# Second layer: turning the mixed rows of tiles 4 to 11 on VectorE and through DRAM instead of on TensorE

## The chip, the cores and the metric

The kernel runs on one core of one Trainium2 chip. The core has five engines that run their own instruction streams in program order: TensorE (PE in the rows), VectorE (DVE), ScalarE (ACT), GpSimd (POOL) and SyncE (SP), which here only issues DMAs. ScalarE can issue DMAs too. Transfers run on 16 DMA engines, beside the compute engines. The metric is the device time of one execution in microseconds (us); lower is better.

## What is computed

The reference chains three layers over 1536 rows (2 batches of 768) of width 512: a retention attention, a mixture of 8 experts with two experts for each row, and the layer that the change touches, called the second layer here. Cut to what matters, with `x` the weighted sum of the two experts' results for each row:

```python
x = top2_w[:, 0, None] * y0 + top2_w[:, 1, None] * y1      # the mixed rows
h = x @ w_in                                               # 512 -> 1024
e = np.exp(h - h.max(-1, keepdims=True))
solu = h * e / (e.sum(-1, keepdims=True) + 1e-9)
ln = (solu - mean(solu)) / np.sqrt(var(solu) + 1e-6) * g_ln
out = ln @ w_out                                           # 1024 -> 512
```

All of it is float32; the kernel gets there by splitting each operand into a high and a low part and adding three products.

## The kernel before

The second layer works on 12 tiles of 128 rows (`NT = 12`). For tile i it takes these steps, each a small function:

- `gather(i)`: GpSimd fetches the two experts' rows of the tile by two indirect DMAs from `yg` into `y0` and `y1` (L801).
- `mix(i)`: ScalarE scales `y0` (L811), VectorE adds the scaled `y1` (L812); the result `t` has a row of the tile in each partition.
- `x2_t(i)`: TensorE turns `t` by four 128x128 transposes into PSUM (L821), so that the width lies in the partitions; ScalarE writes the high part `x2h` (L824), VectorE the low part `x2l` (L825).
- `h_in(i, s)`, s = 0 and 1: 24 matmuls of 512 columns in all, `h` into PSUM bank pair `d` (L840). The first two matmuls read `x2h`, the third reads `x2l`.
- `solu_max(i)`: VectorE takes the row maximum (L845) and negates it (L846). `solu(i)`: ScalarE's exponential (L853), VectorE's product (L854), three short steps, and `z` (L859).
- `z_turn(i)`: VectorE turns the 32x32 blocks of `z` (L904, into `zs`); four DMAs on SyncE's queue store `zs` to DRAM (`zd`, L907); a fifth, behind them on the same queue, loads it back with the blocks in their places (`zc`, L909). It can start when the four stores have landed. Tiles 0 and 11 are turned on TensorE instead (`z_t`, L893).
- `z_parts(i)`: ScalarE and VectorE make the high and low parts `zh` and `zl` from `zc` (L916, L917).
- `RS[i]()`: ScalarE's sum of squares (L864) and six short GpSimd steps for the row's scale.
- `out_mm(i)`: 24 matmuls of 512 columns (L950), 16 with `zh` first. `store_out(i)`: ScalarE scales and evacuates (L956, tile `o`), SyncE stores to the output (L957).

The order of every engine's instructions is the order in which the program calls these functions; no scheduler moves them. An instruction that waits holds what stands behind it on its engine, and a DMA that waits holds its queue. A prologue brings the first tiles in; then a loop runs over i = 1 to 11. Its body before the change, cut to the calls, with the tile that each works on:

```python
store_out(i - 1); x2_t(i + 3); mix(i + 4); gather(i + 5); z_parts(i)
RS[i + 1]() ; h_in(i + 2, 0); h_in(i + 2, 1)
solu_max(i + 2); solu(i + 2); z_turn(i + 2); out_mm(i)
```

So one pass of the loop gives TensorE the transposes of tile i+3, `h_in` of tile i+2 and `out_mm` of tile i. The prologue ends with `x2_t(3)`, `mix(4)`, `solu_max(2)`, `solu(2)`, `z_turn(2)`, the row scale of tile 1 and `out_mm(0)`.

Of the kernel before, what the change touches and what calls it, by code (L numbers as in the profile page):

```python
# [8 lines left out]
F32 = mybir.dt.float32  # L9
F32R = mybir.dt.float32r  # L10
# [5 lines left out]
AF = mybir.ActivationFunctionType  # L16
# [26 lines left out]
def retnet_moe_solu(ctx, tc, qT, kT, k, v, w_gate, w_noise, noise, w1, w2, w_in, w_out, g_ln,  # L43
                    decay, out, dbg=None):
    nc = tc.nc
# [3 lines left out]
    NT = B * NC  # L49
    E = w1.shape[0]  # L50
    DM = H * D
    KD = DM // 128
# [9 lines left out]
    dram = ctx.enter_context(tc.tile_pool(name="dram", bufs=1, space=DRAM))  # L62
# [10 lines left out]
    def bank(tag, shape=(128, 512)):  # L73
        if tag == "a" and tag not in psum:
            turned[0] ^= 1
            tag = f"a{turned[0]}"
        pool, n = psum[tag]
        return pool.tile(list(shape), F32, tag=tag, name=tag, bufs=n)
# [63 lines left out]
    def row0(i):  # L142
        c, b = order[i]
        return b * S + c * 128
# [646 lines left out]
    Y, X2, X2T, PH, ST, Z, RS, ZT = {}, {}, {}, {}, {}, {}, {}, {}  # L791
# [3 lines left out]
    def gather(i, upto=OFF[-1]):  # L795
        if i >= NT:
            return
        Y[i] = []
        for s in range(2):
            t = fr.tile([128, DM], F32, tag=f"y{s}", name=f"y{s}", bufs=3)  # L800
            nc.gpsimd.indirect_dma_start(  # L801
                out=t, out_offset=None, in_=yg[:upto],
                in_offset=bass.IndirectOffsetOnAxis(ap=slot_y[:, i, s:s + 1], axis=0))
            Y[i].append(t)

    def mix(i):
        if i >= NT:
            return
        y0, y1 = Y.pop(i)
        t = fr.tile([128, DM], F32, tag="t", name="t")  # L810
        nc.scalar.activation(t, y0, AF.Copy, scale=top_w[:, i, 0:1])  # L811
        nc.vector.scalar_tensor_tensor(t, y1, top_w[:, i, 1:2], t, op0=OP.mult, op1=OP.add)  # L812
        X2[i] = t

    def x2_t(i):
        if i >= NT:
            return
        t = X2.pop(i)
        p = bank("a")
        for d in range(KD):  # L820
            nc.tensor.transpose(p[:, d * 128:(d + 1) * 128], t[:, d * 128:(d + 1) * 128], ident)  # L821
        hi = fr.tile([128, KD * 128], F32R, tag="x2h", name="x2h")
        lo = fr.tile([128, KD * 128], F32R, tag="x2l", name="x2l")
        nc.scalar.activation(hi, p, AF.Copy)  # L824
        nc.vector.tensor_sub(lo, p, hi)  # L825
        X2T[i] = (hi, lo)

    def h_in(i, s):
        if i >= NT:
            return  # L830
        if s == 0:
            PH[i] = bank(f"d{i % 2}", (128, 2, 512))
        hi, lo = X2T[i]
        f = slice(s * 512, s * 512 + 512)
        terms = [(x, d, n) for d in range(KD) for x, n in ((hi, 0), (hi, 1), (lo, 0))]
        if s == 0 and i == 0:

            terms.sort(key=lambda t: t[0] is lo)
        for m, (x, d, n) in enumerate(terms):
            nc.tensor.matmul(PH[i][:, s, :], x[:, d * 128:(d + 1) * 128], unit_t[8 * E + d][n][:, 0, f],  # L840
                             start=(m == 0), stop=(m == len(terms) - 1))

    def row_max(pool, ph):
        t = pool.tile([128, 16], F32, tag="st", name="st", bufs=3)
        nc.vector.reduce_max(t[:, 0:1], ph, axis=AX.X)  # L845
        nc.vector.tensor_scalar_mul(t[:, 0:1], t[:, 0:1], -1.0)  # L846
        return t

    def solu_rows(pool, ph, t):

        col = lambda n: t[:, n:n + 1]
        ee = pool.tile([128, FF], F32, tag="ee", name="ee")
        nc.scalar.activation(ee, ph, AF.Exp, bias=col(0), accum_out=col(1))  # L853
        nc.vector.scalar_tensor_tensor(ee, ph, 1.0, ee, op0=OP.mult, op1=OP.mult, accum_out=col(2))  # L854
        nc.vector.tensor_scalar_add(col(1), col(1), 1e-9)
        nc.vector.reciprocal(col(3), col(1))
        nc.vector.scalar_tensor_tensor(col(4), col(2), 1.0 / FF, col(3), op0=OP.mult, op1=OP.mult)
        z = pool.tile([128, FF], F32, tag="z", name="z")
        nc.vector.tensor_scalar(z, ee, col(3), col(4), op0=OP.mult, op1=OP.subtract)  # L859
        return z, lambda: row_scale(ee, z, t)  # L860
# [14 lines left out]
    def solu_max(i):  # L875
        if i >= NT:
            return
        ST[i] = row_max(m2, PH[i].rearrange("p a f -> p (a f)"))

    def solu(i):  # L880
        if i >= NT:
            return
        Z[i], RS[i] = solu_rows(m2, PH.pop(i).rearrange("p a f -> p (a f)"), ST.pop(i))
# [17 lines left out]
    def z_turn(i):  # L901

        t = m2.tile([128, 4, 256], F32, tag="zs", name="zs")
        nc.vector.transpose(t.rearrange("p g c -> p (g c)"), Z.pop(i).rearrange("p (k g c) -> p g k c", g=4, c=32))  # L904
        d = dram.tile([4, 32, 4, 256], F32, tag="zd", name="zd", bufs=3)
        for a in range(4):
            nc.sync.dma_start(d[:, :, a].rearrange("g i c -> i g c"), t[32 * a:32 * a + 32])  # L907
        t = m2.tile([128, 4, KF, 32], F32, tag="zc", name="zc")
        nc.sync.dma_start(t, d.rearrange("g i a (k j) -> (g i) a k j", j=32))  # L909
        ZD[i] = t  # L910

    def z_parts(i):
        hi = m2.tile([128, KF, 4, 32], F32R, tag="zh", name="zh")
        lo = m2.tile([128, KF, 4, 32], F32R, tag="zl", name="zl")
        t = ZD.pop(i).rearrange("p a k j -> p k a j")
        nc.scalar.activation(hi, t, AF.Copy)  # L916
        nc.vector.tensor_sub(lo, t, hi)  # L917
        ZT[i] = tuple(x.rearrange("p k a j -> p (k a j)") for x in (hi, lo))
# [24 lines left out]
    def out_mm(i, c=slice(0, DM), between=None):  # L943
        hi, lo = ZT[i]
        p = bank("b")[:, c]
        terms = [(z, f, n) for z, ns in ((hi, (0, 1)), (lo, (0,))) for f in range(KF) for n in ns]
        for m, (z, f, n) in enumerate(terms):
            if between and m == len(terms) // 2:
                between()
            nc.tensor.matmul(p, z[:, f * 128:(f + 1) * 128], w_rows(f, n)[:, c],  # L950
                             start=(m == 0), stop=(m == len(terms) - 1))
        OUT[i] = p

    def store_out(i, c=slice(0, DM)):
        o = m2.tile([128, DM], F32, tag="o", name="o", bufs=3)
        nc.scalar.activation(o[:, c], OUT.pop(i), AF.Copy, scale=RS[i])  # L956
        nc.sync.dma_start(out[row0(i):row0(i) + 128, c], o[:, c])  # L957

# [128 lines left out]
    for e in range(E - 1):  # L1087
# [5 lines left out]
        for j in range(4):  # L1093
            for f in (2 * j, 2 * j + 1):
                hidden(e, f, slice(0 if e else EARLY, CAPS[e]))
                if f in (1, 3, 4, 5):
                    d = (1, 3, 4, 5).index(f)
# [66 lines left out]
    fr = m2_ctx.enter_context(tc.tile_pool(name="fr", bufs=2, side="right", reuse_waits="tile"))  # L1164
    for b in range(3):
        py = bank(("c0", "c3", "c2")[b])
        c = slice(b * 128, (b + 1) * 128)
# [15 lines left out]
    m2 = m2_ctx.enter_context(tc.tile_pool(name="m2", bufs=2, reuse_waits="tile"))  # L1183
    psum_pool(m2_ctx, "psum2", a=2, b=2, d0=1, d1=1)
    gather(3)
    gather(4)
    h_in(0, 0)
    x2_t(1)
    h_in(0, 1)
    mix(2)  # L1190
    solu_max(0)
    solu(0)
    x2_t(2)
    h_in(1, 0)
    h_in(1, 1)
    mix(3)
# [9 lines left out]
    mix(4)  # L1206
    gather(5)
    solu_max(2)
    solu(2)
    z_turn(2)  # L1210
    RS[1] = RS[1]()
    out_mm(0)

    for i in range(1, NT):
        store_out(i - 1)
        x2_t(i + 3)
        mix(i + 4)
        gather(i + 5)
        if i < NT - 2:
            z_parts(i)  # L1220
        if i + 1 < NT:
            RS[i + 1] = RS[i + 1]()
        h_in(i + 2, 0)
        h_in(i + 2, 1)
        solu_max(i + 2)
        solu(i + 2)
        if i + 2 < NT - 1:
            z_turn(i + 2)
        if i == NT - 3:
            z_parts(i + 1)  # L1230
        if i < NT - 1:
            out_mm(i, between=(lambda: z_t(NT - 1)) if i == NT - 2 else None)
        else:
            for c in (slice(0, DM // 2), slice(DM // 2, DM)):
                out_mm(i, c)
                store_out(i, c)
# [5 lines left out]
    with tc.If(full == 1), ExitStack() as fb_ctx:  # L1242
        fb = fb_ctx.enter_context(tc.tile_pool(name="fb", bufs=1))
        psum_pool(fb_ctx, "psum3", a=2, b=2, d0=1)
        for g in range(NT // 4):
            xT = fb.tile([128, KD, 4, 128], F32, tag="fx", name="fx")
            acc, gate = [], []
            for n in range(4):
                i = 4 * g + n
                x = fb.tile([128, DM], F32, tag="fr", name="fr")  # L1250
                nc.sync.dma_start(x, xd[i * 128:(i + 1) * 128, :])
                p = bank("a")
# [9 lines left out]
                a = fb.tile([128, DM], F32, tag=f"fa{n}", name="fa")  # L1262
# [10 lines left out]
            for e in range(E):  # L1273
                wa, wb = load_w(w1[e], w2[e])
                h = fb.tile([128, KF, 512], F32, tag="fh", name="fh")
                for f in range(KF):
                    p = bank("b")
# [5 lines left out]
                for n in range(4):  # L1283
                    p = bank("a")
# [6 lines left out]
            for n in range(4):  # L1291
                i = 4 * g + n
                x2T = fb.tile([128, DM], F32, tag="fr", name="fr")
                p = bank("a")
# [12 lines left out]
                for f in range(KF):  # L1307
                    p = bank("a", (128, 128))
                    nc.tensor.transpose(p, z[:, f * 128:(f + 1) * 128], ident)
                    nc.vector.tensor_scalar_mul(zT[:, f], p, gcol[:, f:f + 1])  # L1310
                p = bank("b")
                for f in range(KF):
                    nc.tensor.matmul(p, zT[:, f], wb[:, f], start=(f == 0), stop=(f == KF - 1))
                o = fb.tile([128, DM], F32, tag="fo", name="fo")
# [57 lines left out]
```

## Time and profile before

| | us |
|---|---|
| median of 3 runs | 509.22 |
| lowest and highest run | 509.2 and 509.84 |
| the profiled execution | 509.66 |
| span in the profile, first to last instruction | 507.8 |
| TensorE busy, of the span | 499.9 (98%) |
| VectorE busy | 370.9 (73%) |
| ScalarE busy | 214.6 (42%) |
| GpSimd busy | 152.8 (30%) |

The profile is of one execution, 0.44 us above the median; 1.86 us of its time lie around the span. Times in the views are from the span's start. The second layer's first transposes stand at 361 us, and the loop over i runs from 387.1 us to the end. An engine's busy share says how much it works, not whether it is waited for: for that the views to read are the chain of work that ended last, and for each engine the idle time before an instruction with what ended it. DMA issues stand in the rows under the engine whose queue issues them (SPq, ACTq); the time in such a row is that of issuing, not that of the transfer.

### The profile page before, as it was taken

The numbers are of one execution on the slowest core, as the hardware profiler recorded it, in microseconds if no ns is written. First come the engines' busy times: TensorE is split into PE (matmuls) and PEld (weight loads), VectorE is DVE, ScalarE is ACT, GpSimd is POOL, SyncE is SP. The second block draws the span as 40 slices with busy tenths as digits, with TensorE's granted clock in tenths as the row PEclk, the third lists the DMA queues.
The fourth block names the chain that finished last, engine by engine and source line by source line (L and its number), as shares of the span: only waits on it lengthen the run. The fifth ranks groups of instructions, "written<-read, shape, count | busy, mean of one in ns | idle before, by whom it ended". The sixth has DMA issues, their size and how long they took to land.

```text
span 507.8 us, 8812 instructions
## 1 busy us (share of the span) xinstructions
PE 499.9 (98%) x3188; PEld 453.6 (89%) x3188; DVE 370.9 (73%) x744; ACT 214.6 (42%) x424; POOL 152.8 (30%) x225
## 2 busy tenths in 40 slices
PE   9999999999999999999999999999999999999995
PEld 8888888989999999999999999998788888888885
DVE  4578787679789688687889888875288766666540
ACT  5756424244424334423444444354365443344441
POOL 4111111878317127037046000000426442211120
PEclk9999999999999999999999999999999999999999
DMA  8999652977567567766587857664734765533431
GB/s 298 288 342 300 218 180 75 319 234 264 141 222 238 136 216 246 215 221 232 146 257 237 252 172 230 184 174 143 233 100 135 220 198 179 160 103 105 119 110 48
DMA packets 58962, 100.14 MB, mean 197 GB/s; under 512 B 9856, under 2 KB 27264, under 8 KB 58912
## 3 DMA queue, kind: packets, MB, share of 16 engines
q1 hardware_dynamic: 52032, 84.87, 53.4%
q0 software_dynamic: 4992, 13.25, 8.8%
q10 hardware_dynamic: 1888, 1.39, 1.0%
q8 instruction: 27, 0.44, 0.4%
q14 instruction: 23, 0.19, 0.1%
HBM read 76.81 MB, written 22.68 MB: 196 GB/s over the span
## 4 chain that ended last, share of the span: by engine, by line
PE 95%; DVE 3%; DMA 1%; issue 0%; ACT 0%; DVEq 0%; ACTq 0%
PE c L1075 25%; PE b L707 15%; PE d L840 13%; PE b L950 13%; PE a L707 12%; PE c L1173 3%; PE b L403 3%; PE c L457 3%; PE c L445 2%; PE a L431 1%; PE c L420 1%; PE a L821 1%; DMA kt<-in_kT_dram 1%; PE a L1034 0%; DVE hl L712 0%
## 5 line engine op out<-in xcount | busy, mean ns | idle before, releaser
L1021 POOL DMA_INDIRECT xq<-xd,rows x78 | 90.2, 1156 | 96.0 <-DVE xt L1038 73.4
L1075 PE MATMUL c<-hh,wh 128*128 128x448 f32 (+5 forms) x224 | 79.1, 353 | 0.0
L1075 PE MATMUL c<-hl,wh 128*128 128x448 f32 (+5 forms) x224 | 78.9, 352 | 0.0
L1075 PE MATMUL c<-hh,wl 128*128 128x448 f32 (+5 forms) x224 | 78.8, 352 | 0.0
L202 DVE TENSOR_TENSOR wl<-wr,wh 128x1024 fp32r<-128x1024 f32 x64 | 76.7, 1219 | 0.8 <-ACT wh L201 0.8
L201 ACT ACTIVATE wh<-wr 128x1024 fp32r<-128x1024 f32 x64 | 65.4, 1049 | 0.0
L801 POOL DMA_INDIRECT y<-yg,slot_y x24 | 23.5, 978 | 88.0 <-DMA yg<-y 77.3
L1075 PEld LDWEIGHTS c<-hh,wh 128*128 128x128 f32 x224 | 42.2, 188 | 1.3
L1075 PEld LDWEIGHTS c<-hh,wl 128*128 128x128 f32 x224 | 42.1, 188 | 1.2
L1075 PEld LDWEIGHTS c<-hl,wh 128*128 128x128 f32 x224 | 42.1, 188 | 1.2
L1040 ACT ACTIVATE xh<-xt 128x428 fp32r<-128x428 f32 (+5 forms) x24 | 13.0, 540 | 62.0 <-DVE xt L1038 62.0
L711 ACT ACTIVATE hh<-b 128x256 fp32r<-128x256 f32 (+8 forms) x40 | 18.7, 467 | 48.4 <-PE b L707 41.6
L707 PE MATMUL b<-xh,wh 128*128 128x448 f32 (+6 forms) x112 | 39.1, 349 | 0.0
L840 PE MATMUL d<-wh,x2h 128*128 128x512 f32 x96 | 39.0, 407 | 0.0
L707 PE MATMUL a<-xh,wh 128*128 128x448 f32 (+6 forms) x112 | 39.0, 348 | 0.0
L707 PE MATMUL b<-xh,wl 128*128 128x448 f32 (+6 forms) x112 | 38.8, 347 | 0.0
L707 PE MATMUL a<-xh,wl 128*128 128x448 f32 (+6 forms) x112 | 38.8, 347 | 0.0
L840 PE MATMUL d<-wl,x2h 128*128 128x512 f32 x96 | 37.9, 395 | 0.0
L840 PE MATMUL d<-wh,x2l 128*128 128x512 f32 x96 | 37.4, 395 | 0.0
L711 ACT ACTIVATE hh<-a 128x448 fp32r<-128x448 f32 (+6 forms) x28 | 14.3, 512 | 46.7 <-PE a L707 32.7
L853 ACT ACTIVATE ee<-d,st 128x1024 f32<-128x1024 f32 x12 | 13.4, 1114 | 40.4 <-DVE st L846 37.3
L712 DVE SCALAR_TENSOR_TENSOR hl<-b,hh 128x256 fp32r<-128x256 f32 (+8 forms) x40 | 21.0, 524 | 8.2 <-ACT hh L711 6.5
(230 smaller groups left out, 1075.6 us busy)
## 6 DMA issues: line engine op xcount, KB each, us to landing
wr<-in_moe_w_dram SPq DMA_DIRECT2D x62, 512.0 KB
zd<-zs SPq DMA_DIRECT2D x40, 128.0 KB
zc<-zd SPq DMA_DIRECT2D x10, 512.0 KB
raw<-in_moe_w_in_dram SPq DMA_DIRECT2D x8, 512.0 KB
raw<-in_moe_w_out_dram SPq DMA_DIRECT2D x8, 512.0 KB
yg<-yr SPq DMA_DIRECT2D x16, 208.0 KB
qt<-in_qT_dram SPq DMA_DIRECT2D x12, 256.0 KB
vt<-in_v_dram SPq DMA_DIRECT2D x12, 256.0 KB
```

Of the source, the lines that this page charges most:

```text
L201: nc.scalar.activation(hi, t, AF.Copy)
L202: nc.vector.tensor_sub(lo, t, hi)
L403: nc.tensor.matmul(p[s][:, hp, :], KT[i][r, hp, :], QT[i][r, hp, :], start=True, stop=True)
L457: nc.tensor.matmul(rows[:, at:at + 128 + 2 * E], XT[i][:, s, k, :], unit[:, s, k, :], start=(k == 0), stop=(k == 1), skip_group_check=True)
L707: nc.tensor.matmul(p, w[:, 0, f * 128:(f + 1) * 128], x[:, d, c], start=(n == 0), stop=(n == len(terms) - 1))
L711: nc.scalar.activation(hh[:, f, c], p, AF.Relu)
L712: nc.vector.scalar_tensor_tensor(hl[:, f, c], p, 0.0, hh[:, f, c], op0=OP.max, op1=OP.subtract)
L801: nc.gpsimd.indirect_dma_start(out=t, out_offset=None, in_=yg[:upto], in_offset=bass.IndirectOffsetOnAxis(ap=slot_y[:, i, s:s + 1], axis=0))
L840: nc.tensor.matmul(PH[i][:, s, :], x[:, d * 128:(d + 1) * 128], unit_t[8 * E + d][n][:, 0, f], start=(m == 0), stop=(m == len(terms) - 1))
L950: nc.tensor.matmul(p, z[:, f * 128:(f + 1) * 128], w_rows(f, n)[:, c], start=(m == 0), stop=(m == len(terms) - 1))
L1021: nc.gpsimd.indirect_dma_start(out=x[:, b], out_offset=None, in_=xd.rearrange("r (a c) -> (r a) c", a=4), in_offset=bass.IndirectOffsetOnA ...
L1075: nc.tensor.matmul(py[d][:, :CAPS[e]], c, h[:, f, :CAPS[e]], start=(f == 0 and n == 0), stop=(f == KF - 1 and n == 2))
```

## The change

The transposes of `x2_t` leave TensorE for tiles 4 to 11; tiles 0 to 3 keep them. In their place stand four functions, built like `z_turn` and `z_parts`: `x_turn` (VectorE turns the 32x32 blocks of `t` into `xs`), `x_store` (four DMAs on ScalarE's queue, `xs` to DRAM tile `xt`), `x_fetch` (one DMA on SyncE's queue, `xt` to `xc`) and `x_parts` (ScalarE and VectorE make `x2h` and `x2l`, now from SBUF). `xs` and `xc` have one buffer each; `o` loses one of three.

```diff
+    def x_turn(i):
+        t = m2.tile([128, 4, 128], F32, tag="xs", name="xs", bufs=1)
+        nc.vector.transpose(t.rearrange("p g c -> p (g c)"), X2.pop(i).rearrange("p (k g c) -> p g k c", g=4, c=32))
+        XS[i] = t
+    def x_store(i):
+        t = XS.pop(i)
+        d = dram.tile([4, 32, 4, 128], F32, tag="xt", name="xt", bufs=3)
+        for a in range(4):
+            nc.scalar.dma_start(d[:, :, a].rearrange("g i c -> i g c"), t[32 * a:32 * a + 32])
+        XD[i] = d
+    def x_fetch(i):
+        t = m2.tile([128, 4, KD, 32], F32, tag="xc", name="xc", bufs=1)
+        nc.sync.dma_start(t, XD[i].rearrange("g i a (k j) -> (g i) a k j", j=32))
+        XD[i] = t
+    def x_parts(i):
+        hi = fr.tile([128, KD, 4, 32], F32R, tag="x2h", name="x2h")
+        lo = fr.tile([128, KD, 4, 32], F32R, tag="x2l", name="x2l")
+        t = XD.pop(i).rearrange("p a k j -> p k a j")
+        nc.scalar.activation(hi, t, AF.Copy)
+        nc.vector.tensor_sub(lo, t, hi)
+        X2T[i] = tuple(x.rearrange("p k a j -> p (k a j)") for x in (hi, lo))
...
     def store_out(i, c=slice(0, DM)):
-        o = m2.tile([128, DM], F32, tag="o", name="o", bufs=3)
+        o = m2.tile([128, DM], F32, tag="o", name="o", bufs=2)
...
     solu_max(2)
+    x_turn(4)
     solu(2)
+    x_store(4)
     z_turn(2)
+    x_fetch(4)
     RS[1] = RS[1]()
     out_mm(0)
 
     for i in range(1, NT):
         store_out(i - 1)
-        x2_t(i + 3)
         mix(i + 4)
         gather(i + 5)
         if i < NT - 2:
             z_parts(i)
+        x_turn(i + 4)
         if i + 1 < NT:
             RS[i + 1] = RS[i + 1]()
+        x_store(i + 4)
         h_in(i + 2, 0)
         h_in(i + 2, 1)
         solu_max(i + 2)
+        x_parts(i + 3)
         solu(i + 2)
+        x_fetch(i + 4)
         if i + 2 < NT - 1:
             z_turn(i + 2)
```

SyncE's queue, from the turn of tile 1 in the prologue to the first stores of tile 3 in the loop's first pass. Before (`zd` and `zc` are the DRAM copy of `z` and its way back, `out_dram` the output):

```order
L907 DMA zd<-zs 32x4x256 x4
L909 DMA zc<-zd 128x1024
L907 DMA zd<-zs 32x4x256 x4
L909 DMA zc<-zd 128x1024
L957 DMA out_dram<-o 128x512
L907 DMA zd<-zs 32x4x256 x4
```

and now, the same stretch (`xc<-xt` is `x_fetch`, first of tile 4, then of tile 5):

```order
L943 DMA zd<-zs 32x4x256 x4
L945 DMA zc<-zd 128x1024
L943 DMA zd<-zs 32x4x256 x4
L945 DMA zc<-zd 128x1024
L851 DMA xc<-xt 128x512
L993 DMA out_dram<-o 128x512
L851 DMA xc<-xt 128x512
L943 DMA zd<-zs 32x4x256 x4
```

The fetch of tile 4 stands behind the stores and the load of `z` of tile 2; the fetch of tile 5 stands behind the first output store and ahead of the stores of tile 3.

ScalarE, from the exponential of tile 2 in the prologue to the exponential of tile 3 in the loop's first pass. Before (`ee,st<-d` is the exponential, `ee,st<-z` the sum of squares, `t<-y` the first half of `mix`):

```order
L853 ACTIVATE ee,st<-d_4401,st 128x1024
L864 ACTIVATE ee,st<-z 128x1024
L956 ACTIVATE o<-b,st 128x512
L824 ACTIVATE x2h<-a 128x512
L811 ACTIVATE t<-y_4445,top_w 128x512
L916 ACTIVATE zh<-zc 128x1024
L864 ACTIVATE ee,st<-z 128x1024
L853 ACTIVATE ee,st<-d_4531,st 128x1024
```

and now:

```order
L889 ACTIVATE ee,st<-d_4401,st 128x1024
L844 DMA xt<-xs 32x4x128 x4
L900 ACTIVATE ee,st<-z 128x1024
L992 ACTIVATE o<-b,st 128x512
L811 ACTIVATE t<-y_4445,top_w 128x512
L952 ACTIVATE zh<-zc 128x1024
L900 ACTIVATE ee,st<-z 128x1024
L844 DMA xt<-xs 32x4x128 x4
L860 ACTIVATE x2h<-xc 128x512
L889 ACTIVATE ee,st<-d_4538,st 128x1024
```

The stores of tile 4 stand ahead of the sum of squares of tile 1, those of tile 5 behind the sum of squares of tile 2, and the high part of tile 4, which reads the fetched `xc`, stands ahead of the exponential of tile 3.

## Rows read from the trace of the kernel before

**Rows 1.** The page: the chain that ended last, by engine.
```profile
PE 95%; DVE 3%; DMA 1%; issue 0%; ACT 0%; DVEq 0%; ACTq 0%
```

**Rows 2.** Chain in order of time, loop's start and last transposes: start, us, work.
```profile
387.10 0.44 PE a L821 x4
...
393.13 5.50 PE b L950 x24
398.63 0.44 PE a L821 x4
399.07 5.59 PE d L840 x24
...
467.83 0.44 PE a L821 x4
```

**Rows 3.** Timeline of SyncE's DMA issues: start, us, line, transfer, count.
```profile
392.03 1.74 SPq L907 DMA_DIRECT2D zd<-zs  x4
397.13 0.34 SPq L909 DMA_DIRECT2D zc<-zd  x1
...
422.92 1.76 SPq L907 DMA_DIRECT2D zd<-zs  x4
426.62 0.34 SPq L909 DMA_DIRECT2D zc<-zd  x1
...
484.30 0.34 SPq L909 DMA_DIRECT2D zc<-zd  x1
```

**Rows 4.** Timeline of ScalarE: loop's first two passes, and tile 10's parts.
```profile
386.94 1.12 ACT L853 ACTIVATE ee<-d,st 128x1024 f32<-128x1024 f32 x1 [4.04 <-DVE st L846]
388.05 1.05 ACT L864 ACTIVATE ee<-z 128x1024 f32<-128x1024 f32 x1
...
390.75 1.06 ACT L916 ACTIVATE zh<-zc 128x1024 fp32r<-128x1024 f32 x1
...
402.16 1.06 ACT L916 ACTIVATE zh<-zc 128x1024 fp32r<-128x1024 f32 x1 [1.65 <-DMA zc<-zd]
...
488.19 1.06 ACT L916 ACTIVATE zh<-zc 128x1024 fp32r<-128x1024 f32 x1 [0.40 <-DMA zc<-zd]
```

**Rows 5.** Timeline of ScalarE at the kernel's start: first of four DMA issues, next instruction.
```profile
0.74 0.41 ACTq L237 DMA_DIRECT2D kt<-in_kT_dram  x1
...
2.71 1.28 ACT L336 ACT_TABLE_LOAD   x1 [2.71 <-issue]
```

**Rows 6.** Timeline of VectorE: tile 2 in the prologue, then one steady pass.
```profile
386.69 0.15 DVE L846 TENSOR_SCALAR st<-st 128x1 f32<-128x1 f32 x1
...
390.75 1.25 DVE L904 STREAM_TRANSPOSE zs<-z 128x1024 f32<-128x1024 f32 x1
...
430.60 1.23 DVE L854 SCALAR_TENSOR_TENSOR ee<-d,ee 128x1024 f32<-128x1024 f32 x1 [1.35 <-ACT ee L853]
...
433.18 1.25 DVE L904 STREAM_TRANSPOSE zs<-z 128x1024 f32<-128x1024 f32 x1
```

**Rows 7.** Groups by line, 398.6 to 479.4 us: busy us, mean ns, idle before.
```profile
L917 DVE TENSOR_TENSOR zl<-zc,zh 128x1024 fp32r<-128x1024 f32 x7 | 8.6, 1226 | 2.4 <-ACT zh L916 2.4
```

**Rows 8.** Stretches: length, busy PE, PEld, DVE, ACT, POOL, PEclk, DMA share, GB/s.
```profile
8.00:12.00 4.00, 4.00 (x70) 3.54 (x66) 2.14 (x4) 3.87 (x19) 0.79 (x2) 1.00 1.04 388
387.10:398.63 11.53, 11.53 (x54) 9.40 (x53) 8.86 (x17) 6.95 (x12) 7.54 (x16) 1.00 0.62 181
```

**Rows 9.** Stretches after TensorE's last matmul, the same columns.
```profile
502.60:505.20 2.60, 0.00 (x0) 0.00 (x0) 0.00 (x0) 0.45 (x1) 0.00 (x0) 1.00 0.19 63
505.40:507.80 2.40, 0.00 (x0) 0.00 (x0) 0.00 (x0) 0.00 (x0) 0.00 (x0) 0.50 0.01 3
```

**Rows 10.** Timeline of TensorE: first matmuls, and the same 16 later.
```profile
1.05 3.38 PE L264 MATMUL c<-ones 128*128 128x128 bf16 x30 [1.05 <-DVE ones L261]
4.59 2.08 PE L403 MATMUL b<-qt,kt 64*128 64x128 f32 x16 [0.15 <-DMA kt<-in_kT_dram]
...
17.64 1.16 PE L403 MATMUL b<-qt,kt 64*128 64x128 f32 x16
```

More of the change, by code (lines that the diff above doesn't have):

```diff
@@ L826, in x2_t @@
         X2T[i] = (hi, lo)
+    XS, XD = {}, {}
+    def x_turn(i):
+        if i >= NT:
+            return
+        t = m2.tile([128, 4, 128], F32, tag="xs", name="xs", bufs=1)
+        nc.vector.transpose(t.rearrange("p g c -> p (g c)"), X2.pop(i).rearrange("p (k g c) -> p g k c", g=4, c=32))
+        XS[i] = t
+    def x_store(i):
+        if i >= NT:
+            return
+        t = XS.pop(i)
[4 more added lines that the diff above has]
+    def x_fetch(i):
+        if i >= NT:
+            return
+        t = m2.tile([128, 4, KD, 32], F32, tag="xc", name="xc", bufs=1)
+        nc.sync.dma_start(t, XD[i].rearrange("g i a (k j) -> (g i) a k j", j=32))
+        XD[i] = t
+    def x_parts(i):
+        if i >= NT:
+            return
+        hi = fr.tile([128, KD, 4, 32], F32R, tag="x2h", name="x2h")
[4 more added lines that the diff above has]
+        X2T[i] = tuple(x.rearrange("p k a j -> p (k a j)") for x in (hi, lo))
     def h_in(i, s):
```

## The prediction

> **What bounds the kernel now.** I read first the chain that ended last. TensorE has 95% of it [rows 1]: work taken from TensorE can shorten the kernel, and a TensorE wait lengthens it, one for one. Next, the same chain in order of time over the second layer [rows 2]: the reader should see matmuls standing end to end, with 0.44 us of transposes between one pass's `out_mm` and the next pass's `h_in`. From the loop's start on TensorE waits for nothing; a pass is 0.44 + 5.59 + 5.50 = 11.53 us. Then the queues of the engines that will feed `h_in` instead: SyncE's issues [rows 3], ScalarE [rows 4] and VectorE [rows 6].
>
> **What is removed.** Eight groups of transposes, the first at 387.10 and the last at 467.83 [rows 2], leave TensorE: 8 x 0.435 = 3.5 us, all on the path. A pass becomes 11.09 us. ScalarE's and VectorE's reads of the turned tile from PSUM are replaced by equal-sized reads from SBUF.
>
> **What is added, in the steady passes.** VectorE gets a turn of 512 columns, half of the 1.25 us of `zs` [rows 6], 0.63 us; ScalarE gets four DMA issues. Its only four issues in a row took from 0.74 to 2.71 us, when the next instruction came [rows 5]; SyncE's four `z` stores took 1.74 [rows 3]. I take 1.9 us. The order now ties VectorE and ScalarE into a ring: turn 0.63, stores 1.9, `x2h` 0.6 (a little over half of the 1.06 of `zh` [rows 4]), exponential and its hand-over 1.2 [rows 4], then from VectorE's product to the end of `zs` 433.18 + 1.25 - 430.60 = 3.83 [rows 6], `mix` 0.75 (half of its columns, so between half and all of `zl`), `zl` 1.23 [rows 7]: 10.1 us, under the 11.09 of TensorE. So this hides, by 1 us a pass, and lateness from the first tile is made good at that rate. `x2l` (0.65, half of `zl` and a little) fits beside the exponential. The fetch of tile i+4 has a whole pass until its parts are made, and SyncE would be free for it: between the load of `z` at 426.62 and the next `z` stores a pass after 422.92, at 434.45, stands one output store [rows 3]. The lost buffer of `o` costs nothing: a store issued in one pass has two passes, 22 us, to land.
>
> **What is added, for the first tile.** Tile 4 has no such slack. Its fetch stands on SyncE behind the stores and the load of `z` of tile 2, and the load waits until the stores have landed. The stores are issued at 392.03, when `zs` of tile 2 is written [rows 3, 6]; nothing moves that forward, as the turn of tile 4 (386.84 to 387.5) fits into VectorE's wait for the exponential. The load came 5.1 us after the first store there and 3.7 us in a steady pass [rows 3], so at 395.7 to 397.1. I take 396.0: the sum of squares of tile 1 now starts behind the four store issues, 387.5 + 1.9 = 389.4 instead of 388.05 [rows 4], which delays GpSimd's row scale and the gather behind it, out of the way of the `z` stores. From the issue of that load to ScalarE's use of it, where ScalarE was waiting, took 484.30 to 488.19, 3.9 us, and 397.13 to 402.16, 5.0 us [rows 3, 4]; I take 4.2. The fetch is 256 KB behind it on the same queue: 0.7 us at 388 GB/s, 1.45 at the 181 GB/s of that pass [rows 8]; I take 1.0. So `x2h` of tile 4 starts at 400.3 to 403.6, taken 401.2.
>
> TensorE would be ready for `h_in` of tile 4 at 398.63 - 0.44 = 398.2 [rows 2]. It starts at 401.2 + 0.6 = 401.8, a pause of 3.6 us; its third matmul needs `x2l`, at 402.45, and 22 x 0.233 us later it ends at 407.6. Before it ended at 399.07 + 5.59 = 404.66 [rows 2]: +2.9 us (+2.0 to +5.3 from the ends). Six later groups of transposes still fall away, -2.6. Net +0.3 us, with ends -0.6 and +2.7.
>
> Behind the waiting `x2h` on ScalarE stand the exponential of tile 3, `o`, `mix` and `zh` of tile 2; four instructions of at most 1.12 us [rows 4] end by 406.3, and `out_mm` wants `zh` at 407.6. It is hidden, and so is the product of tile 3 on VectorE, which nobody on TensorE needs in this pass. The `zh` of tile 1, which ended at 391.81 [rows 4], moves to some 392.7 (1.35 for the stores, less 0.5 for the `x2h` that is gone); `out_mm` wants it at 393.13 - 0.44 = 392.69 [rows 2]. A wait of up to 0.7 us there falls into the later one.
>
> [...]
>
> **The sum.** +0.3 + 1.2 = +1.5 us. The profiled execution, 509.66 us with 1.86 around its span of 507.8, becomes 511.2; it lies 0.44 over the median of 509.22, so on the median's scale the forecast is **510.7 us**.
>
> **The rivals.**
> *The clock holds*: the same pause, but the full clock stays, as it did through the 2.6 us to 505.2 [rows 9]. 509.22 + 0.3 = 509.5 us, from 508.6 to 511.9.
> *The fetch isn't held behind the load* (faster): if SyncE's second transfer is served beside the first, it needs only what the steady `z` stores needed after their last issue, 426.62 - 424.68 = 1.9 us [rows 3]. Issued at 396.35, it lands at 398.3, `x2l` is there at 399.55, `h_in` ends at 404.7: 0.0 - 2.6 = -2.6, **506.7 us**. From 399.9 on, the start of `x2h` decides: before that the kernel is faster by over 1 us. Against it: the ends of the wait in [rows 4] are for a load of 512 KB that goes first. [...]
> *The ring gets longer than the pass* (slower still): from four issues of over 2.9 us, 0.73 each, ScalarE's stores hold `x2h` and the exponential in every pass. The four issues that the trace has took 1.97 us together [rows 5]; at twice that, 3.9, a pass is 12.1 us and seven passes lose 7 us more than the forecast, 517.7. Half of that excess gives **514 us**.
> That the change doesn't do what it says can be left out: in the built order the transposes of tiles 4 to 11 are gone from TensorE.
>
> **How the numbers follow.** Forecast, pause with a fallen clock: 0.45. Clock holds: 0.30. Fetch served early: 0.12. Longer ring or a later fetch than my ends: 0.13. The range 508.3 to 513.4 leaves out most of the third and half of the fourth. A difference of 0.2%, 1.0 us, is about what a measurement of this kernel can tell from no change. Under 508.2: the third case, 0.12. Between 508.2 and 510.2: most of the second, 0.24, and the early end of the first, 0.05: 0.29. Above: 0.59.
>
> **What would show it.** In the profile after: no L821 from the loop's start; passes of 11.1 us from tile 5's `h_in` on, without idle on TensorE. One idle stretch on TensorE of some 3.6 us ahead of `h_in` of tile 4, with ScalarE's `x2h` of tile 4 waiting for the DMA of `xc` until about 401, and SyncE's fetch issued right behind the load of `zc` near 396. A granted clock under 1.00 for a few microseconds behind it. Wrong if TensorE doesn't wait there (then 505.7), if it waits for VectorE or ScalarE in later passes too, or if the stores on ScalarE take over 2.9 us.

## The result and the profile after

| | before | after |
|---|---|---|
| median, us | 509.84 (7 runs) | 513.88 (7 runs, 512.76 to 514.74) |
| ratio to the kernel before | | 1.007, 95% interval 1.0046 to 1.0093 |
| the profiled execution, us | 509.66 | 513.03 |
| its span, us | 507.8 | 511.3 |
| second layer: end of `out_mm` of tile 0 to the start of ScalarE's last `o`, us | 115.5 | 118.1 |
| start of ScalarE's last `o` to the end of the span, us | 5.2 | 6.5 |

The kernel became slower, in the direction of the forecast and by more: 4.0 us between the medians where 1.5 was forecast; by the ratio 3.6 us, between 2.3 and 4.7. One of the seven executions before (531.71 us) and, below, the profiled one of e6_between_pad140 (610.98 us, mean granted clock 0.754) were in a slower state; the ratios leave such executions out, and of that profile only SyncE's jump is read. A second measurement of the same kernel, e5_after below, gives 1.0096 (1.0074 to 1.0117). The profiled execution is among the quicker ones, 0.85 us under its median.

The steady passes came out as forecast. The chain of the kernel after in order of time, from the end of tile 4's `h_in` on (start, us, work):

```profile
409.50 5.50 PE b L986 x24
415.00 5.59 PE d L876 x24
...
481.56 5.59 PE d L876 x24
487.16 8.24 PE b L986 x36
```

The transposes of [rows 2] are gone, a pass is 11.09 us, and nothing stands between the pieces up to tile 10. From the end of `h_in` of tile 4 to the start of the last `o` it is now 95.28 us and was 97.92: 2.64 us less, the six groups of the forecast (2.6).

The loss stands in two other places. The first is tile 4. All waits of TensorE from 384 us on (what waits, for what: us in total, times, longest):

```profile
PE d L876 <- ACT x2h L860: 4.0, 1, 4.0
PE b L986 <- ACT zh L952: 0.2, 1, 0.2
```

The chain there:

```profile
396.59 4.95 DMA xc<-xt
...
401.57 0.64 ACT x2h L860
...
402.25 7.25 PE d L876 x24
```

SyncE's issues of the load and of the fetch, and ScalarE's rows (in brackets the idle time before, and what ended it):

```profile
395.87 0.10 SPq L945 DMA_DIRECT2D zc<-zd  x1
396.59 0.01 SPq L851 DMA_DIRECT2D xc<-xt  x1
```

```profile
387.09 0.83 ACTq L844 DMA_DIRECT2D xt<-xs  x2
...
387.95 1.14 ACTq L844 DMA_DIRECT2D xt<-xs  x2
389.14 1.06 ACT L900 ACTIVATE ee<-z 128x1024 f32<-128x1024 f32 x1 [1.40 <-issue]
...
394.34 1.81 ACTq L844 DMA_DIRECT2D xt<-xs  x4
401.57 0.63 ACT L860 ACTIVATE x2h<-xc 128x512 fp32r<-128x512 f32 x1 [8.10 <-DMA xc<-xt]
```

Against [rows 3, 4] the reader sees that the load of `z` of tile 2 is issued where it was before, with the fetch right behind it, and that ScalarE waits 8.10 us, to the end, for that fetch. The granted clock around the pause (stretch: length, busy PE, PEld, DVE, ACT, POOL, PEclk, DMA share, GB/s):

```profile
392.30:397.80 5.50, 5.32 (x23) 4.41 (x24) 3.11 (x4) 1.16 (x3) 4.47 (x10) 1.00 0.79 197
397.80:402.20 4.40, 0.45 (x2) 0.02 (x1) 0.00 (x0) 0.63 (x2) 2.31 (x4) 0.97 1.01 370
402.25:405.70 3.45, 3.45 (x9) 2.71 (x10) 2.94 (x7) 3.17 (x5) 0.00 (x0) 0.55 0.40 121
405.70:409.50 3.80, 3.80 (x18) 3.08 (x17) 3.77 (x5) 1.15 (x2) 2.20 (x3) 1.00 0.35 79
```

Behind the pause the granted clock is 0.55 over 3.45 us, into which only 9 matmuls fit, and 1.00 over the next 3.80; `h_in` takes 7.25 us instead of 5.59.

The second place is the end of the program. SyncE's waits behind the last load, of the kernel before and then of the kernel after; each is a jump over the fallback code that is left out, seen as SyncE's idle time before the next instruction of its own:

```profile
SPq L1242 <- SPq L1242: 0.8, 2, 0.5
```

```profile
SPq L1284 <- SPq L1284: 2.7, 1, 2.7
```

Between the two tails of the table lie 1.3 us, and the experiments on the jump below show that they belong to it.

### The profile page after: what moved, and what is told of

Same layout as the page of the kernel before. It is cut to its first block, busy times and chain, and to the rows that moved or that the text cites. A ratio compares the mean times of both kernels' runs of the same rounds, so it can differ in the third digit from the quotient of the medians.

```text
span 511.3 us, 8843 instructions
## 1 busy us (share of the span) xinstructions
PE 498.0 (97%) x3156; PEld 451.1 (88%) x3156; DVE 375.6 (73%) x752; ACT 216.0 (42%) x424; POOL 152.8 (30%) x225
## 4 chain that ended last, share of the span: by engine, by line
PE 89%; DVE 5%; issue 2%; DMA 2%; ACT 1%; SPq 0%; ACTq 0%; DVEq 0%
PE c L1111 25%; PE b L707 16%; PE a L707 12%; PE b L986 11%; PE d L876 10%; PE c L1209 3%; PE b L403 3%; PE c L457 3%; PE c L445 2%; PE a L431 1%; PE c L420 1%; DMA xc<-xt 1%; DMA kt<-in_kT_dram 1%; DVE ee L890 1%; DVE st L881 1%
## 5 line engine op out<-in xcount | busy, mean ns | idle before, releaser
L1057 POOL DMA_INDIRECT xq<-xd,rows x78 | 87.7, 1124 | 96.2 <-DVE xt L1074 73.7
L903 POOL TENSOR_SCALAR st<-st 128x1 f32<-128x1 f32 x12 | 3.0, 249 | 80.8 <-ACT ee L900 80.7
## 6 DMA issues: line engine op xcount, KB each, us to landing
wr<-in_moe_w_dram SPq DMA_DIRECT2D x62, 512.0 KB
zc<-zd SPq DMA_DIRECT2D x10, 512.0 KB
raw<-in_moe_w_in_dram SPq DMA_DIRECT2D x8, 512.0 KB
raw<-in_moe_w_out_dram SPq DMA_DIRECT2D x8, 512.0 KB
```

Of the source, the lines that this page charges most:

```text
L1057: nc.gpsimd.indirect_dma_start(out=x[:, b], out_offset=None, in_=xd.rearrange("r (a c) -> (r a) c", a=4), in_offset=bass.IndirectOffsetOnA ...
```

## The experiments

Each experiment was timed against the kernel before on the same chip. "x2h" is TensorE's wait before tile 4's `h_in`, "h_in" the length of that `h_in`, "place" the place of SyncE's jump (the number of instructions ahead of it in SyncE's built program), "jump" SyncE's idle time at it, and "tail" the time from the start of ScalarE's last `o` to the end of the span. x2h, h_in, jump and tail are in us and of one profiled execution.

| run | median | before | ratio (95%) | x2h | h_in | place | jump | tail |
|---|---|---|---|---|---|---|---|---|
| kernel before | 509.22 | | | 0 | 5.59 | 511 | 0.5 | 5.2 |
| kernel after | 513.88 | 509.84 | 1.0070 (1.0046 to 1.0093) | 4.0 | 7.25 | 530 | 2.7 | 6.5 |
| e1_fetch_ahead | 507.92 | 509.48 | 0.9976 (0.9957 to 0.9994) | 0 | 5.60 | 529 | 2.8 | 6.5 |
| e2_filler | 512.92 | 509.48 | 1.0061 (1.0043 to 1.0080) | 0.7 | 6.13 | 530 | 2.5 | 6.3 |
| e3_fetch_between | 507.22 | 509.48 | 0.9951 (0.9933 to 0.9970) | 0 | 5.59 | 530 | 2.7 | 6.5 |
| e4_before_pad | 509.99 | 509.48 | 1.0009 (0.9997 to 1.0021) | 0 | 5.59 | 530 | 2.5 | 6.3 |
| e5_after | 514.14 | 509.15 | 1.0096 (1.0074 to 1.0117) | 4.4 | 8.45 | 530 | 2.5 | 6.3 |
| e6_between_pad140 | 505.50 | 509.15 | 0.9930 (0.9911 to 0.9948) | | | 670 | 0.5 | |
| e7_between_pad60 | 505.56 | 509.15 | 0.9937 (0.9919 to 0.9954) | 0 | 5.59 | 590 | 0.5 | 4.4 |
| e8_tile4_tensor | 507.61 | 509.15 | 0.9976 (0.9963 to 0.9990) | 0 | 5.59 | 527 | 2.7 | 6.5 |
| e9_after_pad8 | 514.54 | 510.78 | 1.0078 (1.0047 to 1.0109) | 4.4 | 7.68 | 538 | 2.2 | 6.3 |
| e10_after_pad4 | 515.63 | 510.78 | 1.0110 (1.0074 to 1.0146) | 5.5 | 7.30 | 534 | 2.6 | 6.4 |
| e11_only_tile4 | 516.19 | 510.78 | 1.0089 (1.0059 to 1.0119) | 3.1 | 7.28 | 515 | 0.5 | 5.6 |
| e12_filler_pad8 | 513.13 | 510.78 | 1.0056 (1.0026 to 1.0085) | 0.7 | 6.13 | 538 | 1.9 | 6.0 |
| e13_after_early60 | 512.23 | 509.26 | 1.0056 (1.0036 to 1.0076) | 5.8 | 8.18 | 590 | 0.5 | 4.4 |
| e14_after_late8 | 514.18 | 509.26 | 1.0096 (1.0075 to 1.0116) | 4.3 | 8.01 | 538 | 2.2 | 6.3 |

Up to the second layer's loop profiled executions differ by up to 2.4 us (`out_mm` of tile 0 ends at 385.85 in e7_between_pad60 and at 388.23 in e2_filler), in work that is the same in all; lengths of the loop are therefore counted from that end, and times compared by their ratios.

### Which part costs: tile 4 against tiles 5 to 11

**e8_tile4_tensor.** Tile 4 stays on TensorE, tiles 5 to 11 are turned.

```diff
-    x_turn(4)
     solu(2)
-    x_store(4)
     z_turn(2)
-    x_fetch(4)
...
         store_out(i - 1)
+        if i == 1:
+            x2_t(4)
...
-        x_parts(i + 3)
+        if i > 1:
+            x_parts(i + 3)
```

> Tile 4 stays on TensorE, as in the kernel before; only tiles 5 to 11, which have a whole pass for their way through DRAM, are turned by VectorE. My theory (the whole loss comes from tile 4's wait and from the end of the program): no wait of TensorE before h_in of tile 4, seven groups of transposes of 0.435 us fall away, 3.05 us; the last ScalarE output at about 499.5; with a long jump the time is 507.7, with a short one 506.4. The jump leads here to a place 4 instructions ahead of where the changed kernel's does, so this run also narrows where the block ends. Rival (the ring of VectorE and ScalarE costs something in every pass): TensorE waits in several passes and the time stays over 508.5.

Measured 507.61 us. TensorE waits for nothing from 380 us on; the loop to the last `o` takes 112.40 us where the kernel before took 115.48, 3.08 less, against the 3.05 of seven groups. The median fell by 1.5 us, less than that by about the longer jump. The ring of VectorE and ScalarE costs nothing in the steady passes.

**e11_only_tile4.** The other half: tile 4 alone goes through DRAM.

```diff
         store_out(i - 1)
-        x2_t(i + 3)
+        if i > 1:
+            x2_t(i + 3)
...
+        if i == 1:
+            x_parts(4)
         solu(i + 2)
```

> The kernel before, with tile 4 alone turned by VectorE through DRAM as the change does it; tiles 5 to 11 stay on TensorE. The jump is at place 515, so the end of the program is as before. My theory of tile 4 in the changed kernel: 4.0 to 4.4 us of waiting for x2h, 1.4 to 1.7 us for matmuls at the lower clock and 0.25 for x2l, less 0.435 for its transposes: 5.2 to 5.9 us over the kernel before, 514.4 to 515.0 where that takes 509.2. Rival (part of the pause is taken back in later passes, where TensorE waits for nothing before): under 513.

Measured 5.4 us over the kernel before, inside the forecast of 5.2 to 5.9; the ratio's interval is wider, 3.0 to 6.1 us. In the profiled execution the loop takes 120.45 us instead of 115.48, 5.0 more, and the tail 0.4 more. TensorE's wait for `x2h` is 3.1 us there, less than the 4.0 to 4.4 expected. SyncE's idle time at the jump is as short as before.

```profile
402.69 0.64 ACT x2h L860
403.33 0.04 issue
403.37 7.28 PE d L876 x24
```

In this chain `h_in` of tile 4 is long again, 7.28 us. Nothing of it is taken back later: behind it the chain goes on with pieces of 5.50 and 0.44 us, as before. The two halves, +5.4 and -1.5 us, make +3.9; the change measured +4.0 and +5.0, so they add up as closely as these measurements agree.

**e5_after** is the changed kernel once more, as a control.

> The changed kernel itself, beside the kernels of this call. Every theory expects its earlier ratio, 1.007 (513.9 us where the kernel before takes 509.8), with TensorE waiting about 4.0 us for ScalarE's x2h of tile 4, the first matmuls of the next pass near half the clock, and an idle time of about 2.7 us at SyncE's jump over the fallback code.

The wait was 4.4 us, and `h_in` took 8.45. Over the profiled executions of this fetch order the wait was 3.1 to 5.8 us where nothing filled it: its size varies by more than any of the other terms.

### What holds the fetch

**e1_fetch_ahead**: the fetch goes on SyncE's queue ahead of tile 2's stores and load.

```diff
     x_store(4)
-    z_turn(2)
     x_fetch(4)
+    z_turn(2)
```

> The changed kernel with one line moved in the prologue: the fetch of tile 4 stands on SyncE's queue ahead of the z stores and the z load of tile 2 instead of behind them. Theory (TensorE's pause ahead of h_in of tile 4 comes from the fetch's place in the queue): the fetch is issued at about 391.5 us, ScalarE's x2h of tile 4 no longer waits for it, TensorE goes from out_mm of tile 1 to h_in of tile 4 without a pause, the granted clock stays at 1.00, and against the changed kernel 4.2 us of pause, 0.25 us of waiting for x2l and 1.4 us of clock go away: about 508.0 us where the changed kernel has 513.9, some 0.4% under the kernel before. Rival (the pause comes from the extra traffic of the stores on ScalarE's queue, or from ScalarE's time): a pause of 2 us or more stays, 511 us or more.

**e3_fetch_between**: it goes between tile 2's four stores and its load, where SyncE stood waiting anyway.

```diff
-    z_turn(2)
-    x_fetch(4)
+    z_turn(2, lambda: x_fetch(4))
...
             nc.sync.dma_start(d[:, :, a].rearrange("g i c -> i g c"), t[32 * a:32 * a + 32])
+        between()
         t = m2.tile([128, 4, KF, 32], F32, tag="zc", name="zc")
```

> The changed kernel with the fetch of tile 4 between the four z stores of tile 2 and the z load behind them: it no longer waits for the stores to land nor for the load of 512 KB, but still stands behind the stores. Theory (the landing wait and the load ahead of it make the fetch late): it is issued at 393.4 us and ScalarE's x2h of tile 4 can start by about 397, before TensorE asks for it at 398: no pause, 508 us as with the fetch ahead. Rival (the fetch takes its 5 us from issue in any place, since the transfers of that stretch crowd each other): x2h starts at 398.4 or later, a pause of 1 us or more stays, 509 us or more.

Both remove the pause and make the kernel faster than the kernel before: 507.92 and 507.22 us. SyncE's issues in e3_fetch_between, and the fetch in its chain:

```profile
391.17 1.75 SPq L943 DMA_DIRECT2D zd<-zs  x4
393.33 0.34 SPq L851 DMA_DIRECT2D xc<-xt  x1
395.18 0.34 SPq L946 DMA_DIRECT2D zc<-zd  x1
```

```profile
393.33 2.85 DMA xc<-xt
```

The fetch leaves 3.3 us earlier than in the kernel after (2.8 counted from the loop's start) and takes 2.85 us instead of 4.95 to 7.27. The load of `z` waited for its stores until 395.18 in any case. In this execution `out_mm` waits 0.2 us for `zh`, as in the kernel after, and 0.4 us once more two passes later; e7_between_pad60, with the same order, has no such wait. So the place in SyncE's queue was the cause of the pause, as the forecast's argument on the first tile had it. Both runs move the fetch ahead of the load and issue it earlier; no run separates the two.

What made the fetch so long behind the load is read from one row, not shown by a run. Queues of the kernel after from 396 to 402 us (packets, MB, share of the 16 DMA engines' time) and what was issued:

```profile
DMA packets 1084, 1.99 MB, mean 331 GB/s; under 512 B 135, under 2 KB 519, under 8 KB 1084
...
q1 hardware_dynamic: 432, 1.05, 47.8%
q0 software_dynamic: 220, 0.74, 35.1%
q10 hardware_dynamic: 432, 0.20, 11.2%
...
xc<-xt SPq DMA_DIRECT2D x1, 256.0 KB
out_dram<-o SPq DMA_DIRECT2D x1, 256.0 KB
xt<-xs ACTq DMA_DIRECT2D x1, 64.0 KB
y<-yg,slot_y POOLq DMA_INDIRECT x3
```

The DMA engines are full there (share 1.01 from 397.8 to 402.2, above). Beside the load and the fetch they carry an output's store, 0.74 MB of GpSimd's gathers and 0.20 MB of tile 5's own stores, which the change issues at 394.34. The gathers were there before the change too (0.54 MB from 397 to 403 us), these stores were not. The rate of 331 GB/s lies between the 181 and 388 that the forecast took its ends from; there was more to carry than the 768 KB that it counted.

### The clock

**e2_filler**: 16 matmuls of 128x512 between `out_mm` of tile 1 and `h_in` of tile 4, their result unused. **e12_filler_pad8** is the same on top of e9_after_pad8, so that both have the same jump and the same session.

```diff
             out_mm(i, between=(lambda: z_t(NT - 1)) if i == NT - 2 else None)
+            if i == 1:
+                keep_busy(16)
```

> The changed kernel with 16 matmuls of 512 columns added on TensorE between out_mm of tile 1 and h_in of tile 4, into a PSUM bank that nobody reads: 16 x 0.23 = 3.7 us of work that fits into the pause of 4.2 us. Theory (the pause lowers the clock, and that costs 1.4 us on top of the pause): the granted clock stays at 1.00, h_in of tile 4 takes 5.9 us from its first matmul instead of 7.25, and the kernel gets 1.4 us shorter than the changed one, 512.5 us. Rival (the slow h_in is the wait for x2l or slow reads, not the clock): h_in stays at 7.2 us and the time at 513.9.

> e9_after_pad8 with 16 matmuls of 128x512 on TensorE in the pause ahead of h_in of tile 4 (their result is not used), as in e2_filler. Against e9_after_pad8 of this call: if the chip lowers the clock because TensorE idles there, the first matmuls of h_in of tile 4 run at 1.00 or near it and the median falls by 0.7 to 1.5 us, to 511 to 512; if the lower clock has another cause, it stays where it was. The wait that is left in front of x2h can't be gained by this.

e2_filler was compared with the kernel after across sessions, and its 512.92 against 513.88 left that open. Within one session 514.54 became 513.13: the fall of 1.4 us is inside the expected 0.7 to 1.5, the time is over the expected 511 to 512, because e9_after_pad8 itself was slower than expected. The intervals of the two ratios overlap, so the size rests on the rows. The first stretch of tile 4's `h_in`, of e9_after_pad8 and then of e12_filler_pad8 (columns as above):

```profile
403.04:406.50 3.46, 3.46 (x9) 2.45 (x10) 2.95 (x7) 3.17 (x5) 0.00 (x0) 0.62 0.34 97
```

```profile
403.33:406.50 3.17, 3.17 (x13) 2.29 (x14) 2.67 (x7) 3.17 (x5) 0.00 (x0) 1.00 0.38 115
```

With TensorE busy through the pause the clock stays at 1.00 and `h_in` takes 6.13 instead of 7.68 us. So the lower clock follows from the idle time, and it costs some 1.5 us here (7.68 - 6.13; 1.4 by the medians).

### The jump at the end

**e4_before_pad**: the kernel before with 19 empty drain instructions on SyncE ahead of the last expert, which puts its jump at place 530.

```diff
+    for _ in range(19):
+        nc.sync.drain()
     e = E - 1
     hidden_of(e)
```

> The kernel before with 19 empty instructions (drains with nothing to wait for) on SyncE ahead of the last expert, where SyncE waits anyway, so that SyncE's program is as long as that of the changed kernel. Theory (the last 1.3 us of the loss lie behind the last result: SyncE's jump over the fallback code at the kernel's end lands, by the length of its program, in code that isn't loaded yet, 2.7 us of idle instead of 0.5 and 0.7): 1.3 us slower than the kernel before, with the idle of 2.7 us on SyncE at the jump. Rival (the longer end comes from the new transfers or buffers): the same time as the kernel before, and an end of 5.2 us behind ScalarE's last instruction.

The jump went from 0.5 to 2.5 us and the tail from 5.2 to 6.3, without any part of the change. In the median only 0.5 us of it are seen, and the interval ends at 1.07 us: less than the 1.3 expected. The row settles the cause, the median not the size.

**e6_between_pad140** and **e7_between_pad60**: e3_fetch_between with 140 and 60 drains in the pass of the last tile but one.

```diff
+        if i == NT - 2:
+            for _ in range(140):
+                nc.sync.drain()
         if i == NT - 3:
```

> The fetch of tile 4 between the stores and the load of tile 2, as in e3_fetch_between, and 140 empty drain instructions on SyncE in the pass of the last tile but one, where SyncE has nothing to do. They move the jump over the fallback code and the code it jumps to on by 140 places in SyncE's program, so that both lie in one block of code again if the block ends where the two earlier programs put it. Theory (the long jump is the loading of the block of code that the jump leads to): the idle time at the jump falls from 2.7 to about 0.5 us, the time from e3_fetch_between's 507.2 to about 505.7 (between 505.0 and 506.5). Rival (a longer program on SyncE makes the jump longer): the idle time stays at 2.5 to 2.8 us or grows, the time at 507.2.

> The same with 60 empty drains instead of 140: the jump then still leads over the presumed end of a block. Theory of the block of code: the idle time at the jump stays at 2.5 to 2.8 us and the time at 507.2. If it is only the drains that shorten the jump, as work that keeps SyncE awake: 0.5 us and 505.7 here too.

Both jumps were short, and both medians fell to 505.5, from 507.22 in another session; the ratios (0.9930 and 0.9937, after 0.9951) fell by less, and their intervals overlap. The second is a miss: by the theory that was expected there, 60 drains should not have helped. Two readings remained: it is the place of the jump that decides, in another way than by that theory; or drains shortly before the jump help. **e9_after_pad8** and **e10_after_pad4** (8 and 4 drains where e4_before_pad has 19), **e13_after_early60** (60 there) and **e14_after_late8** (8 where e7_between_pad60 has 60), all on the changed kernel, tell them apart.

> The changed kernel with 8 empty drains on SyncE ahead of the last expert of the first layer, 100 us before the end; nothing else differs. They put the jump over the fallback code at place 538 of SyncE's program instead of 530. [...] Rival (drains shorten the jump only where they stand shortly before it): 2.5 us or more, 514.

> The same with 4 drains, the jump at place 534. [...] Rival (any added instruction does it): 0.5 us and 512.5.

> The changed kernel with 60 empty drains on SyncE ahead of the last expert, 100 us before the end, which put the jump at place 590 as in e7_between_pad60, whose drains stood 20 us before the end. Theory (the place in the program decides; the block with the jump's target is asked for about 2.5 us before it is there, at a place between 530 and 538): idle time at the jump 0.5 us, and ScalarE's last output to the end of the span 4.2 to 4.5 us instead of 6.3 to 6.5, the median 2 us under the changed kernel's 514, at 511.5 to 512.5. Rival (drains shortly before the jump are what helps): 2.2 to 2.7 us of idle time and 514.

> The changed kernel with 8 drains in the pass of the last tile but one, 20 us before the end; the jump at place 538, as in e9_after_pad8, where the 8 drains stood 100 us before the end and the idle time was 2.2 us. Theory of the place: 1.9 to 2.3 us again, the time at 513.5 to 514.5. Rival (late drains help): 0.5 us, 512.

SyncE's own waits at the jump, in e10_after_pad4, e9_after_pad8, e14_after_late8 and e13_after_early60:

```profile
SPq L1286 <- SPq L1286: 2.6, 1, 2.6
```

```profile
SPq L1286 <- SPq L1286: 2.2, 1, 2.2
```

```profile
SPq L1287 <- SPq L1287: 2.2, 1, 2.2
```

```profile
SPq L1286 <- SPq L1286: 0.7, 2, 0.5
```

Where the drains stand doesn't matter, the place of the jump does: 60 early ones shorten it, 8 late ones don't, and in one session the two medians lie 1.95 us apart (512.23 and 514.18). At place 538 e9_after_pad8 took 2.2 us and 514.54 us, where I had expected 0.5 us and 512.0 to 512.8 us; e10_after_pad4, at place 534, took 2.6 us, so that an added instruction as such doesn't shorten the jump, and 515.63 us, with a wait for `x2h` of 5.5 us.

By place, the jump took 0.5 us at 511 and 515, 2.5 to 2.8 us at 527 to 534, 2.2 us at 538 (1.9 in e12_filler_pad8), and 0.5 us at 590 and 670. In the trace of the kernel before the jump is at 504.07, 16 instructions run behind it, and the next, at place 664 of SyncE's program, comes at 506.63, 2.56 us behind the jump and after a stop of 0.65 us; in the kernel after the jump is at 506.27, its target lies beyond place 664, and it comes at 509.02, 2.74 us behind.

What SyncE waits for in this time no run shows; that it is code which isn't loaded yet, and that code comes in blocks, was my assumption. The page of the kernel after has a queue for instructions (packets, MB, share of the 16 DMA engines' time):

```profile
q14 instruction: 24, 0.20, 0.1%
```

Two of its packets, 0.02 MB, and one of the other such queue, q8, run between 506.3 and 509.0 us, in SyncE's wait at the jump. Which engine's code a packet holds the profile doesn't show.

## Why the prediction failed in size

Two steps of the prediction failed: the term from the issue of the load to `x2h` was too small (5.2 us, measured 5.7 and, as the median of nine executions, 6.1), and the end of the program, which the change makes 1.3 us longer, was put at nothing without a reason. The parts of the sum in order:

*What was removed*: right. Six groups, 2.64 us for 2.6; e8_tile4_tensor gives 3.08 for seven.

*The steady ring*: right. No wait of TensorE behind tile 4. ScalarE's four stores took 1.8 to 2.0 us for seven of the eight tiles (forecast 1.9). For one, at 441.44, they took 3.10 us, over the 2.9 that the prediction named as a sign of being wrong; TensorE did not wait for it. So one late pass is absorbed; what 3.1 us in every pass would cost, no run shows:

```profile
441.44 3.10 ACTq L844 DMA_DIRECT2D xt<-xs  x4
```

*Hidden work behind the pause* (exponential, `mix`, `zh`, VectorE's lateness): right; none of it is in TensorE's waits but 0.2 us for `zh`, which the pause swallows.

*The issue of the load, 396.0*: right within 0.3 us: 395.87, in a loop that starts 0.41 us earlier.

*From that issue to `x2h`, 4.2 + 1.0 = 5.2 us*: **the first term that was too small**. It took 5.70 us in the profiled execution and 5.7 to 7.8, median 6.1, over the nine profiled executions that keep this order. I had taken the 4.2 between two loads of the kernel before, in whose stretches the DMA engines were 0.71 and 0.74 busy, and added the fetch at an average rate; the row of the queues shows them full (1.01), with gathers and with the stores that the change itself adds for tile 5. That this made the difference is argued from the row.

*The clock, 1.2 us*: the case (it falls) was right: 0.55 was granted over the 3.45 us behind the pause. No run shows the term of 1.2 us as the sum takes it; it was my estimate, and [rows 10] don't give it: the 16 matmuls took 2.08 us early and 1.16 us later, but the profile shows a clock of 1.00 in both stretches (4.59 to 6.67 and 17.60 to 18.80 us). What the runs showed in its place: with the pause filled and the clock at 1.00 `h_in` of tile 4 took 6.13 us (e2_filler and e12_filler_pad8); against that the 7.25 of the kernel after are 1.1 us more, and over the executions with an unfilled pause it was 1.1 to 2.3 us more. That 1.2 came near the 1.1 is luck. The 6.13 are also 0.5 us more than the 5.59 of other tiles, where the forecast allowed 0.2 for the wait for `x2l`; that this wait is the whole of the 0.5 no run shows. The rival that the clock holds is refuted by the 0.55 of the kernel after, and e12_filler_pad8 shows that the idle time lowers it (1.00 instead of 0.62).

*Nothing at the end of the program*: **the step that was missing**. The prediction looked at the engines' work and at SyncE's DMA issues, and took the tail as given. The change adds 19 instructions to SyncE's program, which moves its jump from place 511 to 530, and there the jump takes 2.7 us instead of 0.5: 1.3 us of the tail, outside every term and every rival.

For the profiled execution the accounts close: 513.03 - 511.2 = 1.83, of which the earlier loop -0.41, the later start of `h_in` +0.86 (402.25 + 0.41 for 401.8), `h_in` +0.25 (7.25 for 5.8 + 1.2), the tail +1.26, and -0.1 from the rest. The median lies another 0.85 us higher; executions with a longer pause (4.3 to 5.8 us in five others) fit that. The range ended at 513.4, since its slow end was set by TensorE's pause and clock and had no room for a term that TensorE does not show.

The rival that the fetch isn't served behind the load (506.7) was wrong as the kernel was written; moving the fetch ahead of the load, as e3_fetch_between does, gives 507.22, and 505.56 where the jump is short as well (e7_between_pad60), which is 0.9937 (0.9919 to 0.9954) of the kernel before and, with the 505.50 of e6_between_pad140, the best found.

## What to carry to other kernels

When work is moved to another engine's path through memory, ask what the first of the moved pieces finds in the queue ahead of it: here the seven later pieces gained what was forecast (3.08 us), and the first one lost more than all of them gained (5.0 us in the loop of e11_only_tile4), until its transfer was put into the gap in which the queue stood waiting for stores. Size a transfer by everything that the DMA engines carry in that stretch, as the row of the queues suggests here (1.99 MB in 6 us, where 768 KB had been counted), including what the change itself issues for the next piece. And compare the ends of the two programs too: 19 empty instructions on SyncE, off the critical path, lengthened the jump there from 0.5 to 2.5 us and the tail from 5.2 to 6.3 (e4_before_pad).

## What the runs showed of the hardware that I had not expected

SyncE's jump over 136 instructions took 0.5 us or 2.5 to 2.8 us by nothing but the number of instructions ahead of it (511 and 515 against 527 to 534), and 60 empty instructions, which cost nothing that can be seen, brought back 1.95 us of the median against 8 of them. TensorE's granted clock was 0.55 over the 3.45 us behind the pause of 4.0 us in the kernel after, and 0.62 over the 3.46 us behind that of 4.4 us in e9_after_pad8; with matmuls in the pause it was 1.00 (e2_filler, e12_filler_pad8). And the same 256 KB took 2.85 us ahead of a load of 512 KB (e3_fetch_between) and 4.95 to 7.27 us behind it.
